# Shorter planned reservations on ScalarE and VectorE, and later planned normalisation for batches 4 to 7

## The chip, the cores and the metric

One core of one Trainium2 chip runs the kernel as one launch. The metric is the device time of that launch in microseconds (us). Timed runs are summed up by their median. One further execution was taken by the hardware profiler, and the rows below come from it.

## The reference, cut to what matters

The computation is an attention without softmax, normalised by a root mean square, followed by two feed-forward blocks. Everything is float32.

```python
kv  = einsum('bhsd,bhse->bhde', k, v)            # 8 batches, 8 heads, 576 tokens, 64 wide
out = einsum('bhsd,bhde->bhse', q, kv)
out = out / sqrt(mean(out * out, -1) + 1e-6) * g_norm
x = out.transpose(0, 2, 1, 3).reshape(4608, 512)
h = x @ w_in;  x = maximum(0.01 * h, h) @ w_out          # first block, 512 -> 2048 -> 512
h = x @ w_in2; return (h - tanh(h)) @ w_out2             # second block, the same sizes
```

## The kernel before

**Stages.** The four large products are done in float16 on TensorE: each operand is split into a high and a low part, and three partial products are added (`three`, L639). Around that sits a scheme that makes a 2 by 2 block product out of seven products instead of eight; it needs sums and differences of operand blocks. After a start of about 60 us, TensorE goes through four stages: `up` of block 1 (eight superblocks of 576 tokens, one for each batch, 56 products each), `down` of block 1, `up` of block 2 and `down` of block 2. Within the first `up` stage the attention of batches 2 to 7 is put between the products, one batch well ahead of the superblock that needs it. A product is counted as one slot; superblock b begins at slot 56 b.

**What an `up` product leaves behind.** ScalarE copies intermediate sums out of PSUM (`keep`, L696, tiles `c`, `u` and a block of `g`), VectorE adds the others (`add`, L707). A PSUM bank is free for a later product only after that, so a late copy on ScalarE holds TensorE up. ScalarE then applies the leaky function to a whole tile `g` (L1265), and it is stored.

**What attention leaves behind.** `pair` computes two heads: `kv` on TensorE (`pk`), copied by ScalarE to `kvd` (L967); q transposed (`pq`), copied by ScalarE to `qt` (L986); the product `po` (L997); its square by ScalarE (L1003) and a copy by VectorE to `xg` (L1012). After the last pair of a batch `norms` runs: ScalarE takes the root (L1056), VectorE the reciprocal (L1064), SyncE stores the result and loads it back spread over the partitions into a tile `bc` (L1067, L1073), twice a batch (kk = 0 and 1). GpSimd multiplies `xg` by `bc` in four pieces for each kk (L1079). Then `left_stages` makes the operands: ScalarE writes the high part `opa` (L576), VectorE its low part (L583), GpSimd four sums (L616), then ScalarE `ops` (L576) and VectorE its low part.

**Other work in the same stretch.** Weights of later stages are converted (`convert`: L432 on ScalarE, L436 to L456 on VectorE) and split (`split_late`: GpSimd sums L498 and L502 on `unit`, ScalarE L518, VectorE L521, tiles `wo`).

**What sets the order.** Every engine executes its instructions in the order in which the kernel emits them. That order is not the order of the loops: a planner (`Plan`) keeps a clock of its own, puts each step on a heap under its planned time and emits the heap in that order. For ScalarE ("A"), VectorE ("V") and GpSimd ("G") it keeps lists of taken stretches. `fit` looks for the first place from time t on where a step of length `dur` goes in, and may overlap its neighbour by `over`. `do` books a single step, mostly the copies out of PSUM, without overlap. `chain` books a row of steps one after another; a step that names no engine only waits, such as a load with the time until it is expected to have landed. The planned end of a step is t + `dur` in both, and `chain` adds `HAND`, 0.25 us. A dry pass over the plan finds products planned before their operands and delays them in the plan. The planned lengths stand in the code, such as 0.438 us for a 288-wide copy out of PSUM on ScalarE (width/1000 + 0.15), 0.486 us for the addition on VectorE (1.2 x width/1000 + 0.14), 1.29 us for the low part of four blocks of 288 on VectorE, 0.79 us for a sum on GpSimd of `xg`.

The plan's clock begins at 0 with the kernel. Its products are set to begin at START, 59.9 us by the constants (the load order and 3 x 6.0 - 3.0), plus what the dry pass adds.

Of the kernel before, what the change touches and what calls it, by code (L numbers as in the profile page):

```python
# [29 lines left out]
NOP = 7  # L30
# [18 lines left out]
class Plan:  # L49
# [2 lines left out]

    HAND, OVER = 0.25, {"A": 0.6, "V": 0.35, "G": 0.35}

    def __init__(self, delays, dry):
# [9 lines left out]
    def fit(self, eng, t, dur, over=0.0):  # L67


        taken = self.taken[eng]  # L70
        k = max(0, bisect.bisect(taken, (t, 0.0)) - 1)
        while k < len(taken) and taken[k][0] < t + dur - over:
            t = max(t, taken[k][1])
            k += 1
        while k < len(taken) and taken[k][0] < t:
            k += 1
        taken.insert(k, (t, t + dur))
        return t
# [125 lines left out]
@with_exitstack  # L204
def body(ctx, tc, *args):
    q, out, w1 = args[0], args[-1], args[4]
    sizes = (*q.shape, *out.shape, w1.shape[1])
    pools = {
        "const": ctx.enter_context(tc.tile_pool(name="const", bufs=1)),
        "wpool": ctx.enter_context(tc.tile_pool(name="wpool", bufs=1)),  # L210
        "work": ctx.enter_context(tc.tile_pool(name="work", bufs=1)),
        "dram": ctx.enter_context(tc.tile_pool(name="dram", bufs=1, space=DRAM)),
        "ps": ctx.enter_context(tc.tile_pool(name="ps", bufs=1, space=PSUM)),
    }
    delays = {}
    unseen = Unseen()
    while True:
        late = lay_out(Plan(delays, True), unseen, {n: unseen for n in pools}, sizes, [unseen] * len(args))
        if late is None:
            break  # L220
        delays[late[0]] = delays.get(late[0], 0.0) + late[1]
    with tc.manual_schedule():
        lay_out(Plan(delays, False), tc.nc, pools, sizes, args)


def lay_out(plan, nc, pools, sizes, args):
    q, k, v, g_norm, w1, w2, w3, w4, out = args
    B, H, S, D, NT, DM, DFF = sizes
    NP = DFF // P // 2
# [18 lines left out]
    def bank(n, name):  # L248
        if n in used:
            plan.miss(("bank", n))  # L250
        used.add(n)
        return ps.tile([P, 512], F32, tag=f"p{n}", name=name)

    def free(n):
        used.discard(n)
        plan.met(("bank", n))
# [570 lines left out]
    LOADBC, LOADBC1 = 8.0, 9.0  # L827
# [119 lines left out]
    def pair(b, c, held):  # L947
# [92 lines left out]
        def m_after(e):  # L1040
            if c == PAIRS[-1]:
                norms(b, e)
# [8 lines left out]
    def norms(b, e):  # L1051
        held = {}

        def root():
            held["iv"] = const.tile([4 * Q, T1], F32, tag="iv", name="iv")
            nc.scalar.activation(  # L1056
                out=held["iv"], in_=pm[b][:4 * Q, :T1], func=AF.Sqrt,
                bias=eps_sb, scale=1.0 / (X_SCALE * X_SCALE),
            )
            free(5)  # L1060

        def inverse(n, m=1):
            part = held["iv"][:, CP * n:CP * (n + m)]
            nc.vector.reciprocal(out=part, in_=part)  # L1064

        def store():
            nc.sync.dma_start(out=ivd[b], in_=held["iv"])  # L1067

        def load(kk):
            held[kk] = L.take([P, 4, T1], F32, "bc", True)  # L1070
            rows = ivd[b].rearrange("(w q) t -> q w t", q=Q)
            for h in range(2):
                nc.sync.dma_start(  # L1073
                    out=held[kk].ap[D * h:D * h + D], in_=rows[2 * kk + h:2 * kk + h + 1].broadcast_to((D, 4, T1))
                )

        def scale(kk, e, n0, n1):
            x = xg[b, kk].ap[:, n0:n1]
            e.tensor_tensor(out=x, in0=x, in1=held[kk].ap[:, n0:n1], op=ALU.mult)  # L1079
            if n1 == 4:  # L1080
                L.give(held[kk])

        x0ops[b] = [{}, {}]
        more = []
        for kk in range(2):
            stages = left_stages(
                lambda kk=kk: xg[b, kk].ap, x0ops[b][kk], None, T1, over=lambda kk=kk: L.give(xg[b, kk]), pieces=2,
                first=None if b else "V", rest=None if b else "V", over_s=() if b else (SOVER,),
            )
            if b == 1:  # L1090
                scaled_ = [("V", 0.66, lambda kk=kk, n=n: scale(kk, nc.vector, n, n + 2)) for n in (0, 2)]
            else:
                scaled_ = [("G", 0.76, lambda kk=kk, n=n: scale(kk, nc.gpsimd, n, n + 1)) for n in range(4 if b else 1)]
            more.append([(None, LOADBC if b > 1 else LOADBC1 if b else 6.0, lambda kk=kk: load(kk))] + scaled_ + stages)

        def wide(kk, n):
            k_ = (4 * kk + n) % 4
            if k_ in used:
                raise NoRoom("bank")
            held["b", kk, n] = bank(k_, "pb")  # L1100
            nc.tensor.matmul(
                out=held["b", kk, n][:, :T1], lhsT=hot["t"].ap[:, kk, n], rhs=held["iv"], start=True, stop=True,
            )

        def scale_wide(kk, n):
            x = xg[b, kk].ap[:, n]
            nc.vector.tensor_tensor(out=x, in0=x, in1=held["b", kk, n][:, :T1], op=ALU.mult)
            free((4 * kk + n) % 4)
            if n == 3:
                if kk == 1:  # L1110
                    L.give(hot["t"])
                plan.chain(plan.now + 0.5, more[kk][2:])

        def split():
            if b == 0:
                for kk in range(2):
                    for n in range(4):
                        plan.chain(
                            plan.now + 0.2 + 0.7 * (4 * kk + n),
                            [(None, 0.9, lambda kk=kk, n=n: wide(kk, n)), ("V", 0.46, lambda kk=kk, n=n: scale_wide(kk, n))],  # L1120
                        )
                return
            for kk in range(2):
                plan.chain(plan.now + (4.5 if b > 1 else 1.8) + 3.0 * kk, more[kk])

        end = plan.do("A", e + 0.15, 1.8, root)
        thirds = [("V", 0.7, lambda n=n: inverse(n)) for n in range(T1 // CP)] if b else [("V", 0.7, lambda n=n: inverse(n)) for n in range(3)]
        plan.chain(end + plan.HAND, thirds + ([(None, 0.0, store)] if b else []) + [(None, 0.0, split)])
# [30 lines left out]
    t = 1.0  # L1159
# [77 lines left out]
    FIRST = {1: (None,) * EARLY + (0, 8, 16, 24)[:4 - EARLY], 2: (14, 25, 36, 47), 3: (60, 72, 84, 96)}  # L1237
# [3 lines left out]
    for b in range(1, B):  # L1241
        for hp in range(4):
            c = PAIRS[hp]
            n0 = FIRST[b][hp] if b in FIRST else NOP * (NP * b - 16 + 2 * hp) - 2 * (b - 4)
            if n0 is None:
                continue
            held = ta[b, c][1] if (b, c) in ta else {}
            for (dur, fn, after), o in zip(pair(b, c, held), OFFS.get(b, (1, 4, 6, 8, 10, 13))):
                extra.setdefault(n0 + o, []).append((dur, fn, after))
            if b > 1:  # L1250
                loads.append((n0 - 13, b, c, held))
# [278 lines left out]
```

## Time and profile before

| | |
|---|---|
| median of 3 runs | 1490.52 us (1490.04 to 1491.99) |
| profiled execution | 1495.29 us |
| its span, first to last instruction | 1493.5 us |
| mean granted clock of TensorE in it | 0.986 of full speed |
| TensorE busy | 1443.8 us, 97% of the span |
| VectorE, ScalarE, GpSimd busy | 1245.4, 933.7, 599.8 us |

A busy TensorE is not the same as TensorE at its peak, since matmuls overlap and their ends are modelled; so the waits and the granted clock are read beside the busy time. A time in brackets behind a row of the timeline is the idle time of that engine just before the row, with what ended it.

### The profile page before, as it was taken

The page shows a single profiled execution, that of the slowest core. Times are in us where ns is not written, and L with a number is a line of the kernel's source. Part 1 is how long each engine was busy: PE and PEld are TensorE (multiplying, and loading weights), DVE is VectorE, ACT ScalarE, POOL GpSimd, SP SyncE. Part 2 cuts the span into 40 slices and gives each one's busy share as a digit, 9 for nine tenths or more (in the row PEclk, how much of TensorE's full clock was granted, in tenths as well). Part 3 has the DMA queues.
Part 4 walks back from the last instruction along what each step waited for, and adds up shares of the span by engine and source line. Part 5 has one row for each costly group of instructions (what it writes and reads, how often), then busy time and mean ns, then how long its engine had stood idle before and what let it go on. Part 6 is the DMA issues. An engine that isn't in the chain of part 4 may idle for free. (4 is left out here: it accounts for less than half of the span.)

```text
span 1493.5 us, 32922 instructions
## 1 busy us (share of the span) xinstructions
PE 1443.8 (97%) x12674; PEld 1195.8 (80%) x12674; DVE 1245.4 (83%) x2029; ACT 933.7 (63%) x1529; POOL 599.8 (40%) x614
## 2 busy tenths in 40 slices
PE   5699999999999999999999999999999999999998
PEld 3467777767777777777777888888888888888887
DVE  4896687677877899999996999989999998888871
ACT  5587777778877644444542677768888555555540
POOL 3141340453643444445542111126577444444430
PEclk8799999999999999999999999999999999999999
DMA  9737898899978745555555856646678744444421
GB/s 281 182 105 228 267 298 263 275 327 306 335 260 300 296 166 191 173 173 200 178 172 198 307 211 221 209 172 221 250 253 320 282 143 154 142 143 146 150 86 36
DMA packets 156461, 321.83 MB, mean 215 GB/s; under 512 B 16656, under 2 KB 98448, under 8 KB 156304
## 3 DMA queue, kind: packets, MB, share of 16 engines
q1 hardware_dynamic: 156304, 319.73, 64.7%
q8 instruction: 99, 1.62, 0.4%
q14 instruction: 58, 0.48, 0.1%
HBM read 189.66 MB, written 130.01 MB: 214 GB/s over the span
## 5 line engine op out<-in xcount | busy, mean ns | idle before, releaser
L639 PEld LDWEIGHTS <-w 128*128 128x128 f16 x8400 | 820.1, 98 | 198.1 <-issue 19.2
L616 POOL TENSOR_TENSOR gl<-gl 128x256 f32<-128x256 f32 (+1 forms) x288 | 322.9, 1122 | 368.3 <-DVE gl L616 132.4
L639 PE MATMUL ps_a<-ops,w 128*128 128x288 f16 (+1 forms) x2400 | 331.7, 282 | 6.5 <-ACT c L696 2.8
L639 PE MATMUL ps_c<-ops,w 128*128 128x288 f16 (+1 forms) x2352 | 314.7, 282 | 2.4 <-DVE g L707 2.3
L639 PE MATMUL ps_a<-opa,w 128*128 128x288 f16 (+1 forms) x2016 | 284.6, 281 | 5.6 <-DVE w L521 4.1
L639 PEld LDWEIGHTS <-ops 128*128 128x128 f16 x1728 | 169.1, 98 | 20.0 <-issue 0.4
L639 PE MATMUL ps_b<-opa,w 128*128 128x288 f16 (+1 forms) x1200 | 175.5, 283 | 0.2 <-DVE r_w L344 0.2
L616 DVE TENSOR_TENSOR gl<-gl 128x288 f32<-128x288 f32 (+1 forms) x256 | 142.4, 558 | 4.3
L616 POOL TENSOR_TENSOR x1g<-x1g 128x256 f32<-128x256 f32 x72 | 69.5, 966 | 172.0 <-PE ps_a L639 109.9
L639 PEld LDWEIGHTS <-opa 128*128 128x128 f16 x1296 | 126.8, 98 | 14.7
L576 ACT ACTIVATE ops<-gl 128x1152 f16<-128x1152 f32 x64 | 74.3, 1161 | 96.2 <-POOL gl L616 96.0
L585 DVE SCALAR_TENSOR_TENSOR ops<-gl,inv,ops 128x1024 f16<-128x1024 f32 x72 | 104.3, 1450 | 28.1 <-ACT ops L578 28.0
L578 ACT ACTIVATE ops<-gl,inv 128x1024 f16<-128x1024 f32 x72 | 82.3, 1144 | 65.7 <-POOL gl L616 65.7
L1432 DVE TENSOR_TENSOR g<-g,th 128x512 f32<-128x512 f32 x144 | 111.9, 787 | 0.9 <-ACT th L1428 0.9
L698 ACT ACTIVATE u<-ps_a,up 128x256 f32<-128x256 f32 x144 | 68.1, 473 | 55.0 <-PE ps_a L639 51.3
L583 DVE TENSOR_TENSOR ops<-gl,ops 128x1152 f16<-128x1152 f32 x64 | 94.2, 1475 | 6.9 <-ACT ops L576 6.9
L707 DVE SCALAR_TENSOR_TENSOR g<-ps_c,u 128x288 f32<-128x288 f32 x128 | 57.9, 452 | 49.2 <-PE ps_c L639 48.5
L639 PE MATMUL ps_c<-w,ops 128*128 128x256 f16 x864 | 97.3, 273 | 0.2 <-DVE osb L707 0.2
L639 PE MATMUL ps_a<-w,ops 128*128 128x256 f16 x864 | 95.8, 273 | 0.0
L1079 POOL TENSOR_TENSOR xg<-xg,bc 128x288 f32<-128x288 f32 x48 | 44.8, 961 | 123.8 <-DMA bc<-iv 55.1
L583 DVE TENSOR_TENSOR opa<-gl,opa 128x864 f16<-128x864 f32 x64 | 81.0, 1266 | 2.0 <-ACT opa L576 1.6
L585 DVE SCALAR_TENSOR_TENSOR opa<-gl,inv,opa 128x768 f16<-128x768 f32 x72 | 79.6, 1106 | 0.8 <-ACT opa L578 0.8
(133 smaller groups left out, 2062.3 us busy)
## 6 DMA issues: line engine op xcount, KB each, us to landing
g<-g SPq DMA_DIRECT2D x64, 576.0 KB, 5.1
gl<-g SPq DMA_DIRECT2D x64, 576.0 KB, 4.5
g<-g SPq DMA_DIRECT2D x72, 512.0 KB, 3.4
gl<-g SPq DMA_DIRECT2D x72, 512.0 KB, 4.2
wd<-wo SPq DMA_DIRECT2D x48, 448.0 KB, 3.4
w<-wd SPq DMA_DIRECT2D x24, 896.0 KB, 8.5
words<-in_moe_w_in_dram SPq DMA_DIRECT2D x64, 256.0 KB, 7.1
words<-in_moe_w_out_dram SPq DMA_DIRECT2D x64, 256.0 KB, 4.5
```

The costliest lines, as they stand in the source:

```text
L576: nc.scalar.activation(out=o, in_=i_, func=AF.Copy)
L578: nc.scalar.activation(out=o, in_=i_, func=AF.Identity, scale=scale())
L583: nc.vector.tensor_tensor(out=o, in0=i_, in1=h, op=ALU.subtract)
L585: nc.vector.scalar_tensor_tensor(out=o, in0=i_, scalar=scale(), in1=h, op0=ALU.mult, op1=ALU.subtract)
L616: lambda: e.tensor_tensor(out=g()[:, o], in0=g()[:, a], in1=g()[:, b], op=op),
L639: nc.tensor.matmul(out=out_, lhsT=a, rhs=c, start=start and m == 0, stop=stop and m == n - 1, skip_group_check=not fresh,)
L698: nc.scalar.activation(out=t, in_=src, func=AF.Identity, scale=self.scale)
L707: nc.vector.scalar_tensor_tensor(out=o, in0=src, scalar=self.minus if sub else self.scale, in1=t, op0=ALU.mult, op1=ALU.add,)
L1079: e.tensor_tensor(out=x, in0=x, in1=held[kk].ap[:, n0:n1], op=ALU.mult)
L1432: nc.vector.tensor_tensor(out=o, in0=o, in1=held["t"].ap[:, 2 * n:2 * n + 2], op=ALU.subtract)
```

## The change

The planner's `fit` gets a factor for each engine. From planned time 130 on it books a step on ScalarE for 0.86 and on VectorE for 0.92 of its length, and scales the allowed overlap alike; GpSimd stays at 1. The planned end of the step, which the next step of a chain waits for, still uses the whole length. For batches 4 to 7 `norms` plans each multiplication on GpSimd with 0.95 instead of 0.76 us, and expects the load of `bc` to have landed after 9.5 instead of 8.0 us. The slot at which a batch's attention begins moves from 2 (b - 4) to 3 (b - 4) slots ahead of its base: one slot sooner for batch 5, two for batch 6, three for batch 7, none for batch 4. No instruction is added or taken away; the order of emission changes.

```diff
+    SETTLED, PITCH = 130.0, {"A": 0.86, "V": 0.92, "G": 1.0}
     HAND, OVER = 0.25, {"A": 0.6, "V": 0.35, "G": 0.35}
@@ def fit(self, eng, t, dur, over=0.0):
         taken = self.taken[eng]
+        if t > self.SETTLED:
+            dur *= self.PITCH[eng]
+            over *= self.PITCH[eng]
         k = max(0, bisect.bisect(taken, (t, 0.0)) - 1)
@@ in norms(b, e)
-                scaled_ = [("G", 0.76, lambda kk=kk, n=n: scale(kk, nc.gpsimd, n, n + 1)) for n in range(4 if b else 1)]
-            more.append([(None, LOADBC if b > 1 else LOADBC1 if b else 6.0, lambda kk=kk: load(kk))] + scaled_ + stages)
+                scaled_ = [("G", 0.76 if b < 4 else 0.95, lambda kk=kk, n=n: scale(kk, nc.gpsimd, n, n + 1)) for n in range(4 if b else 1)]
+            more.append([(None, (LOADBC if b < 4 else LOADBC + 1.5) if b > 1 else LOADBC1 if b else 6.0, lambda kk=kk: load(kk))] + scaled_ + stages)
@@ for b in range(1, B): for hp in range(4):
-            n0 = FIRST[b][hp] if b in FIRST else NOP * (NP * b - 16 + 2 * hp) - 2 * (b - 4)
+            n0 = FIRST[b][hp] if b in FIRST else NOP * (NP * b - 16 + 2 * hp) - 3 * (b - 4)
```

## Rows read from the trace of the kernel before

**Rows 1.** Windows, busy time of each engine by stretch, granted clock, DMA share.

```profile
130.00:200.00 70.00, 67.87 (x616) 51.75 (x613) 45.17 (x94) 51.05 (x107) 14.48 (x16) 0.98 0.87 258
200.00:300.00 100.00, 97.56 (x918) 75.09 (x916) 73.39 (x145) 75.38 (x155) 34.36 (x38) 1.00 0.92 279
300.00:400.00 100.00, 96.37 (x867) 73.26 (x865) 79.05 (x138) 81.11 (x162) 58.27 (x68) 0.98 1.01 325
...
600.00:700.00 100.00, 98.80 (x805) 78.54 (x804) 98.80 (x141) 49.55 (x61) 50.43 (x39) 1.00 0.54 180
...
1100.00:1200.00 100.00, 98.06 (x897) 87.49 (x896) 98.40 (x134) 74.55 (x109) 63.54 (x58) 1.00 0.78 284
1200.00:1300.00 100.00, 100.00 (x919) 89.63 (x917) 88.11 (x113) 51.18 (x62) 45.04 (x45) 1.00 0.44 141
```

**Rows 2.** Timeline of GpSimd, batches 4 and 5: multiplications (L1079) and sums.

```profile
257.20 2.56 POOL L1079 TENSOR_TENSOR xg<-xg,bc 128x288 f32<-128x288 f32 x3 [33.89 <-PE pq L976]
265.78 3.80 POOL L1079 TENSOR_TENSOR xg<-xg,bc 128x288 f32<-128x288 f32 x5 [6.02 <-DMA bc<-iv]
269.52 9.11 POOL L616 TENSOR_TENSOR xg<-xg 128x288 f32<-128x288 f32 x8
...
320.05 6.08 POOL L1079 TENSOR_TENSOR xg<-xg,bc 128x288 f32<-128x288 f32 x6 [4.31 <-DMA bc<-iv]
326.08 1.24 POOL L498 TENSOR_TENSOR unit<-unit 128x256 f32<-128x256 f32 x1
```

**Rows 3.** Timeline of all engines at batch 4.

```profile
268.86 0.92 ACT L576 ACTIVATE opa<-xg 128x864 f16<-128x864 f32 x1 [2.29 <-POOL xg L1079]
...
273.55 1.16 ACT L576 ACTIVATE ops<-xg 128x1152 f16<-128x1152 f32 x1 [2.12 <-POOL xg L616]
...
276.66 0.75 PE L997 MATMUL po<-qt,kvd 128*128 128x288 f32 x2 [1.74 <-ACT qt L986]
```

**Rows 4.** The same at batch 5.

```profile
322.93 0.92 ACT L576 ACTIVATE opa<-xg 128x864 f16<-128x864 f32 x1 [3.41 <-POOL xg L1079]
...
324.20 0.90 PE L639 MATMUL ps_a<-ops,w 128*128 128x288 f16 x6 [0.70 <-ACT c L696]
...
328.92 1.04 ACT L518 ACTIVATE wo<-unit,s_w 128x896 f16<-128x896 f32 x1 [0.56 <-POOL unit L502]
...
330.44 1.09 PE L997 MATMUL po<-qt,kvd 128*128 128x288 f32 x2 [1.90 <-ACT qt L986]
```

**Rows 5.** Windows of 5 us, columns as in the first group.

```profile
165.00:170.00 5.00, 3.22 (x13) 2.19 (x13) 3.64 (x7) 4.31 (x10) 4.84 (x7) 0.69 1.06 301
...
330.00:335.00 5.00, 4.56 (x19) 2.90 (x20) 2.99 (x5) 3.67 (x8) 4.84 (x6) 0.66 1.06 392
```

**Rows 6.** Timeline at batch 6.

```profile
391.86 0.90 PE L639 MATMUL ps_a<-ops,w 128*128 128x288 f16 x6 [0.50 <-ACT u L696]
...
397.47 0.75 PE L997 MATMUL po<-qt,kvd 128*128 128x288 f32 x2 [0.54 <-ACT qt L986]
```

**Rows 7.** Timeline at batch 2, and two neighbouring copies on ScalarE.

```profile
165.37 0.92 ACT L576 ACTIVATE opa<-xg 128x864 f16<-128x864 f32 x1 [4.50 <-POOL xg L1079]
...
166.32 0.41 ACT L696 ACTIVATE c<-ps_a 128x288 f32<-128x288 f32 x1
...
166.63 0.40 ACT L696 ACTIVATE u<-ps_a 128x288 f32<-128x288 f32 x1
166.78 1.54 PE L639 MATMUL ps_a<-ops,w 128*128 128x288 f16 x6 [2.13 <-ACT c L696]
```

**Rows 8.** VectorE groups of 520 to 800 us: count, busy, mean ns, idle before.

```profile
L583 DVE TENSOR_TENSOR ops<-gl,ops 128x1152 f16<-128x1152 f32 x52 | 76.8, 1482 | 5.2 <-ACT ops L576 5.2
...
L616 DVE TENSOR_TENSOR gl<-gl 128x288 f32<-128x288 f32 x100 | 58.3, 585 | 1.2
```

**Rows 9.** The same of 130 to 490 us.

```profile
L616 DVE TENSOR_TENSOR gl<-gl 128x288 f32<-128x288 f32 x16 | 7.2, 451 | 0.1
```

**Rows 10.** Timeline: the longest waits of TensorE behind 500 us.

```profile
684.05 3.10 PE L639 MATMUL ps_a<-ops,w 128*128 128x288 f16 x24 [1.20 <-ACT u L694]
...
1155.51 1.47 PE L639 MATMUL ps_c<-ops,w 128*128 128x256 f16 x12 [1.52 <-DVE g L707]
```

**Rows 11.** TensorE, L639 from 60 to 110 us: durations, first and last start.

```profile
L639 PE MATMUL ps_a<-opa,w x60: 283/286/448, 66.6 to 105.9; 128*128 128x288 f16 x60
```

## The prediction, written before the changed kernel was run

> **What bounds the kernel now.** I read the windows first, stage by stage. TensorE is busy 97 to 100% of every stretch behind 130 us, and at the full granted clock nearly everywhere [rows 1]. The reader is to see there that no other engine sets the pace for long, and that what an order can still win is small. The busy time that is missing in the listed windows is 2.13 us up to 200, 2.44 up to 300, 3.63 up to 400, 1.20 from 600 to 700, 1.94 from 1100 to 1200, and nothing from 1200 to 1300. To it comes the clock: it was 0.69 of full speed in the 5 us from 165 and 0.66 in those from 330, both times just behind a wait of TensorE [rows 5]. Full speed is 2.4 GHz and the lower level 1.2 GHz, so these windows mix both. They cost 5 x 0.31 = 1.55 and 5 x 0.34 = 1.70 us. The listed windows and the two clock drops sum to 11.34 + 3.25 = 14.6 us, 1.0% of the time. The start, before 130, is the larger loss, but the change touches it hardly: the factors begin at 130 on the plan's clock, whose products are set for 59.9 us and a little more, where the trace has them from 66.6 on [rows 11]. So 130 on the plan's clock lies some microseconds behind 130 in the trace.
>
> Next I read the timeline around each wait of TensorE in the first stage. They have one pattern. GpSimd's L1079 runs in groups of eight a batch, the first batch being 2; at batch 4 the first three pieces started at 257.20 and the other five only at 265.78, after 6.02 us of waiting for `bc` [rows 2]. ScalarE, in order, had `opa` of that batch at its head and stood 2.29 us for GpSimd, then 2.12 us for `ops` [rows 3]. Behind it in ScalarE's queue stood the copies of `qt` and the copies out of PSUM, and TensorE waited 1.74 us for `qt` [rows 3]. At batch 5 ScalarE stood 3.41 us for `opa`; TensorE lost 0.70 us for the copy `c`, and a little later 1.90 us for `qt`, behind a `wo` step that GpSimd had late [rows 4]; then came the clock drop at 330 [rows 5]. GpSimd had the sums of `unit` behind six multiplications there, and those behind a wait of 4.31 us for `bc` [rows 2]. Batch 6 shows 0.50 and 0.54 us [rows 6]. Batch 2 shows the worst case of the pattern, 4.50 us on ScalarE and 2.13 on TensorE [rows 7].
>
> **The change, part by part.** No instruction comes or goes; all prices are prices of order.
>
> *Riper batches 4 to 7.* In the plan the step `opa` moves by 1.5 us for the load and 4 x (0.95 - 0.76) = 0.76 us for the multiplications, 2.26 us in all, and so do all steps behind it. A copy out of PSUM is planned at its product and stays. So what fell due up to 2.26 us behind `opa` now goes ahead of it on ScalarE. That is as long as the waits of batch 4 (2.29 and 2.12), so I take its 1.74 us as gone. At batch 5 it covers two thirds of the 3.41 us; the copy `c` that TensorE missed by 0.70 us comes ahead: 0.70 gone. On GpSimd the `unit` sums get ahead of some late multiplications and can run in the 4.31 us of waiting; that would free the 1.90 us and its 1.70 us of clock. But the sums on `xg` are still planned at 0.79 us where the eight of batch 4 took 9.11, 1.14 each [rows 2], so crowding behind them stays. The ends are 0 and 3.60; I take half, 1.80. At batch 6 the ends are 0 and 1.04; I take 0.50. What is late next is the operand itself: the multiplications still wait for the same loads, and the low part of `ops` ends no later than it does now unless GpSimd's order worsens. The cover is that superblock 4 begins at slot 224, while the last pair's final step stands at slot 112 + 42 + 13 = 167: 57 slots stand between, against a chain that grows by 2.26 us, three slots. If that cover were gone, TensorE would stand up to 2.26 us a batch, 9 us over four.
>
> *Sooner attention.* It puts back one to three slots for batches 5 to 7. A product takes six passes of 288 columns, planned at 0.735 us, so 0.7, 1.5 and 2.2 us: about what ripening takes. The loads of k, v and q, 13 slots ahead, go out on SyncE's queue that much sooner, with those of `bc` and the stores in the same queue. The DMA share there was 1.01 [rows 1], so they can make a `bc` load later, but only by their own shift. The steps also meet other products of the cycle of seven. Cost: bounded by the waits of such a meeting, a gain of 0.54 or a loss of 0.70 a batch [rows 4, 6], three batches, -1.6 to +2.1. Nothing in the trace says which sign, so I take 0.
>
> *Shorter bookings.* On ScalarE the trace speaks for them: two copies out of PSUM of 0.41 and 0.40 us started 0.31 us apart [rows 7], and the plan books 0.438, now 0.377. The plan comes nearer to the engine. What it moves is steps of other chains forward by some tenths, ahead of or behind a copy. On VectorE it speaks against them for long steps: the low part of 1152 elements took 1.482 us [rows 8] where the plan books 1.29 and now 1.19. Between 600 and 700 and between 1100 and 1200 VectorE is 98% busy [rows 1]; an addition that falls behind such a step comes later. The trace has no row for a changed order. From below, the gain is what stalls remain: batch 2's 2.13 with 1.55 of clock, and the 1.20 and 1.52 us behind 500 us [rows 7, 5, 10], 6.4 us in all. From above, each addition that is newly caught costs 1.20 to 1.52 us [rows 10]. I take 0, since the tight windows with the larger order (the chains begin at the same times, and VectorE's work is the same) have so far just one such wait each.
>
> A rule speaks against this part. A sum of two SBUF tensors of 288 on VectorE took 451 ns in the first stage, when few GpSimd sums ran beside it, and 585 ns on average later [rows 9, 8]: longer beside GpSimd by 30%. The Trainium skill says in "SBUF — State Buffer", section "Who interferes with whom", that a VectorE instruction with two SBUF inputs contends with a GpSimd instruction that reads SBUF, and that the loser of the shared port pair is fully blocked. By that rule a booking of 0.92 would be too short wherever both run; by the rows the sum above stays, and by the rule it would lose what the third rival below loses.
>
> The sum: 1.74 + 0.70 + 1.80 + 0.50 = 4.74 us off 1495.29 (span 1493.5 and 1.8 around it), so 1490.55. That execution is 0.3% above the median of the runs, 1490.52; the ratio 0.9968 put on the median gives 1485.8, and I say 1486.
>
> **The rivals.** *More is freed.* ScalarE's truer bookings also carry the copy `c` of batch 2 ahead of `opa`. For it speaks that 0.31 us distance; against it that `opa` there is ordered by GpSimd's planned times, which don't change for batch 2. All of batches 4 to 6 (1.74 + 0.70 + 3.60 + 1.04 = 7.08) and batch 2 (3.68) would be 10.8 us: 1480.
>
> *The wait only moves.* ScalarE stands for `opa` as before because GpSimd still stands for `bc`, now one other copy behind it. For it: the loads' landing is not changed, and batch 5's 3.41 exceeds 2.26. Then 1.74 goes and 0.70 comes anew at batch 7, which shows no wait now: 1 us off, 1489.5. This is also how it would look if the change did nothing that TensorE feels.
>
> *VectorE's additions fall behind long steps* (the other side). Place: the first `down` stage and the second `up` stage, where VectorE is 98% busy. Price: 1.36 us each (mean of 1.20 and 1.52). From 4.74 / 1.36 = 3.5 of them on the gain is eaten, and from 5.7 on the kernel is slower by over 3 us. One in each of eight superblocks would be 10.9 - 4.7 = 6.2 us slower, 1497. For it: 1.19 booked against 1.482. Against it: the bookings were too short by 0.19 before, and two waits came of it.
>
> **How the numbers follow.** A measurement tells about 0.2%, 3 us, from no change. My forecast gets 0.50 (its own range 1483.4, all of batches 4 to 6, to 1488.5), more freed 0.13, the wait moves 0.20, VectorE's additions 0.17. About 0.05 of the first lies within 3 us. So faster 0.58, same 0.25, slower 0.17. The range takes the forecast, the moved wait, half of more freed and a part of the last: 1481 to 1494.
>
> **What would show each step.** In the profile after: at batches 4, 5 and 6 ScalarE's waits for L1079 and L616 shrink from 2 to 3.4 us to under 1; TensorE's waits for `qt`, `c` and `u` between 265 and 400 us fall from 5.4 us to under 2; the clock drop at 330 is gone. Batch 2's wait stays. The windows from 600 to 700 and from 1100 to 1200 miss no more of TensorE than the 3.1 us of now. I am wrong if waits for L707 or L694 appear in that stretch, if ScalarE stands for `opa` of batches 4 to 7 as long as before, or if batch 7 shows a wait of TensorE for its operands around the start of its superblock.

## The result, and the profile after

The changed kernel took 1503.12 us (median of 4 runs, 1502.16 to 1504.23) against 1491.26 (4 runs) for the kernel before: a ratio of 1.0078, interval 1.006 to 1.0095. It is slower by 0.8%. The forecast was 1486, the range 1481 to 1494. The profiled execution took 1504.01 us with a span of 1502.2; before it was 1495.29 with 1493.5. Behind `fit` line numbers are 4 higher: L707 is L711, and the three lines of `keep` that copy out of PSUM, L696 in the first `up` stage, L694 in the first `down` stage and L698 in block 2, are now L700, L698 and L702.

The windows of the changed kernel, columns as in [rows 1]: stretch and length, then busy time and count of instructions of TensorE, its weight loads, VectorE, ScalarE and GpSimd, then the granted clock, the DMA share and GB/s.

```profile
130.00:200.00 70.00, 67.01 (x621) 51.27 (x620) 47.02 (x95) 49.51 (x107) 14.29 (x16) 1.00 0.87 265
200.00:300.00 100.00, 98.24 (x921) 75.46 (x919) 74.04 (x149) 75.56 (x161) 34.87 (x39) 1.00 0.93 288
300.00:400.00 100.00, 97.68 (x898) 74.54 (x897) 81.81 (x142) 82.18 (x162) 61.28 (x70) 1.00 1.01 323
...
600.00:700.00 100.00, 96.42 (x773) 76.11 (x771) 96.27 (x139) 46.68 (x58) 48.36 (x37) 0.98 0.55 180
700.00:800.00 100.00, 97.03 (x791) 77.08 (x788) 90.12 (x140) 42.29 (x51) 45.33 (x34) 1.00 0.53 179
...
1000.00:1100.00 100.00, 98.46 (x900) 87.80 (x899) 91.00 (x139) 79.24 (x131) 57.87 (x64) 1.00 0.68 242
1100.00:1200.00 100.00, 93.71 (x851) 82.94 (x849) 95.73 (x131) 71.09 (x108) 58.24 (x55) 1.00 0.76 272
1200.00:1300.00 100.00, 100.00 (x919) 89.63 (x917) 85.84 (x112) 50.17 (x61) 43.88 (x44) 1.00 0.49 150
```

Read against [rows 1]: from 200 to 400 the change gains. TensorE misses 4.08 us there where it missed 6.07. From 130 to 200 it misses 2.99 for 2.13, but the granted clock is 1.00 in all three windows up to 400 where two had 0.98. Behind 500 it loses more than that: the windows from 600 to 700 and from 1100 to 1200 miss 3.58 and 6.29 us where they missed 1.20 and 1.94.

What TensorE waited for from 500 to 1190 us in the changed kernel (total, times, longest):

```profile
PE ps_a L643 <- ACT u L702: 4.2, 4, 1.4
PE ps_a L643 <- DVE opa L587: 3.1, 1, 3.1
PE ps_a L643 <- ACT u L698: 3.0, 2, 2.0
PE ps_a L643 <- ACT c L702: 2.6, 2, 2.1
PE ps_c L643 <- DVE g L711: 1.5, 2, 0.9
PE ps_a L643 <- ACT opa L580: 0.5, 1, 0.5
```

That is 14.9 us. The same view of the kernel before sums to 4.8:

```profile
PE ps_c L639 <- DVE g L707: 1.9, 2, 1.5
PE ps_a L639 <- ACT u L694: 1.8, 2, 1.2
PE ps_a L639 <- ACT c L698: 0.6, 1, 0.6
PE ps_a L639 <- DVE r_w L344: 0.5, 1, 0.5
```

The waits that grew name copies out of PSUM on ScalarE (`u` and `c`: 9.8 us for 2.4) and operands (3.6 us, none before). Those for additions on VectorE (`g`) did not grow: 1.5 us for 1.9. One of the new waits in the timeline:

```profile
1135.08 1.48 DVE L589 SCALAR_TENSOR_TENSOR opa<-gl,inv,opa 128x768 f16<-128x768 f32 x1
1135.09 0.82 PE L643 MATMUL ps_a<-opa,w 128*128 128x256 f16 x6
1135.78 1.15 ACT L582 ACTIVATE ops<-gl,inv 128x1024 f16<-128x1024 f32 x1 [1.81 <-POOL gl L620]
1136.48 0.86 DVE L711 SCALAR_TENSOR_TENSOR g<-ps_c,up,u 128x256 f32<-128x256 f32 x2
...
1136.83 0.45 ACT L702 ACTIVATE u<-ps_a,up 128x256 f32<-128x256 f32 x1
...
1137.34 0.81 PE L643 MATMUL ps_a<-ops,w 128*128 128x256 f16 x6 [1.43 <-ACT u L702]
```

ScalarE has the high part `ops` at its head and stands 1.81 us for GpSimd's sums. The copy `u`, which TensorE waits for, is next in line: 1.43 us lost. On VectorE two additions stand behind the low part `opa` of 1.48 us. It is the pattern that the prediction found at batches 2, 4 and 5 in the first stage [rows 3, 4, 7], now in a stage where it was rare. Seven of the eight late copies stand so, behind a step for an operand or a weight that had itself waited for GpSimd, VectorE or a load. Two more of these steps:

```profile
723.99 1.16 ACT L580 ACTIVATE ops<-gl 128x1152 f16<-128x1152 f32 x1 [3.99 <-POOL gl L620]
...
1179.73 0.94 ACT L582 ACTIVATE opa<-gl,inv 128x768 f16<-128x768 f32 x1 [4.44 <-DMA gl<-g]
```

The dearest wait is in the first `down` stage:

```profile
651.28 1.58 DVE L587 TENSOR_TENSOR ops<-gl,ops 128x1152 f16<-128x1152 f32 x1
652.78 1.64 DVE L587 TENSOR_TENSOR opa<-gl,opa 128x864 f16<-128x864 f32 x1
...
654.48 0.77 PE L643 MATMUL ps_a<-opa,w 128*128 128x288 f16 x5 [3.09 <-DVE opa L587]
```

VectorE did another low part first, and TensorE stood 3.09 us for the second one. The two next windows of 5 us show what followed; 165 and 330 stand beside them for [rows 5]:

```profile
165.00:170.00 5.00, 3.66 (x25) 2.52 (x25) 4.93 (x8) 4.90 (x11) 4.76 (x7) 1.00 0.89 309
330.00:335.00 5.00, 5.00 (x61) 4.24 (x62) 5.00 (x6) 3.38 (x8) 4.84 (x6) 1.00 1.08 282
650.00:655.00 5.00, 1.42 (x12) 0.87 (x10) 5.00 (x6) 2.51 (x4) 3.27 (x2) 1.00 0.66 193
655.00:660.00 5.00, 5.00 (x30) 3.35 (x28) 4.97 (x7) 2.22 (x5) 1.99 (x3) 0.66 0.70 235
```

The clock drops at 165 and 330 are gone, and one of the same size has come at 655, worth 5 x 0.34 = 1.7 us. At batch 4 the operands came as the prediction had it:

```profile
265.23 0.91 ACT L580 ACTIVATE opa<-xg 128x864 f16<-128x864 f32 x1
265.46 4.74 POOL L1083 TENSOR_TENSOR xg<-xg,bc 128x288 f32<-128x288 f32 x5 [7.27 <-DMA bc<-iv]
...
269.59 0.91 ACT L580 ACTIVATE opa<-xg 128x864 f16<-128x864 f32 x1
...
274.88 1.16 ACT L580 ACTIVATE ops<-xg 128x1152 f16<-128x1152 f32 x1 [1.29 <-POOL xg L620]
```

GpSimd still stands for `bc`, 7.27 us where it was 6.02 [rows 2], but ScalarE no longer stands with it for `opa` (2.29 us before, [rows 3]), and the wait for `qt` of 1.74 us is gone. Batch 4 has a new one, 1.34 us for an addition at 278.78. At batch 6 ScalarE has a wait for GpSimd that it did not have before, and at 386.52 TensorE stands 0.89 us for a copy `u`:

```profile
383.84 1.16 ACT L580 ACTIVATE ops<-xg 128x1152 f16<-128x1152 f32 x1 [2.81 <-POOL xg L620]
```

### The profile page after: what moved, and what is told of

It is laid out like the page before. It is cut to its first block, busy times and chain, and to the rows that moved or that the text cites. A ratio compares the mean times of both kernels' runs of the same rounds, so it can differ in the third digit from the quotient of the medians.

```text
span 1502.2 us, 32830 instructions
## 1 busy us (share of the span) xinstructions
PE 1442.7 (96%) x12674; PEld 1193.7 (79%) x12674; DVE 1242.2 (83%) x2029; ACT 927.8 (62%) x1529; POOL 607.5 (40%) x614
## 4 chain that ended last, share of the span: by engine, by line
PE 43%; DVE 9%; issue 3%; POOL 2%; ACT 2%; DMA 1%; DVEq 0%; SPq 0%; POOLq 0%; ACTq 0%
PE ps_a L643 20%; PE ps_c L643 13%; PE ps_b L643 6%; PE ps_d L643 4%; DVE opa L587 2%; DVE g L1436 1%; POOL gl L620 1%; DVE g L711 1%; DVE gl L620 1%; DVE opa L589 1%; DVE wo L525 1%; DMA g<-g 1%; ACT ops L580 1%; DVE ops L589 1%; DVE ops L587 1%
## 5 line engine op out<-in xcount | busy, mean ns | idle before, releaser
L620 POOL TENSOR_TENSOR gl<-gl 128x256 f32<-128x256 f32 (+1 forms) x288 | 329.3, 1144 | 374.6 <-DVE gl L620 140.3
L589 DVE SCALAR_TENSOR_TENSOR ops<-gl,inv,ops 128x1024 f16<-128x1024 f32 x72 | 97.6, 1356 | 8.6 <-ACT ops L582 8.6
L702 ACT ACTIVATE u<-ps_a,up 128x256 f32<-128x256 f32 x144 | 67.9, 472 | 48.2 <-PE ps_a L643 46.2
L711 DVE SCALAR_TENSOR_TENSOR g<-ps_c,u 128x288 f32<-128x288 f32 x128 | 57.8, 452 | 44.3 <-PE ps_c L643 38.7
```

The costliest lines, as they stand in the source:

```text
L589: nc.vector.scalar_tensor_tensor(out=o, in0=i_, scalar=scale(), in1=h, op0=ALU.mult, op1=ALU.subtract)
L620: lambda: e.tensor_tensor(out=g()[:, o], in0=g()[:, a], in1=g()[:, b], op=op),
L702: nc.scalar.activation(out=t, in_=src, func=AF.Identity, scale=self.scale)
L711: nc.vector.scalar_tensor_tensor(out=o, in0=src, scalar=self.minus if sub else self.scale, in1=t, op0=ALU.mult, op1=ALU.add,)
```

## The experiments

Theory V: VectorE's factor 0.92 makes the loss. Theory A: ScalarE's factor 0.86 does. Theory O: any new order in the stages behind 500 us costs. Theory R: the riper batches do it. All kernels start from the changed one; 480 and 812 on the plan's clock lie just ahead of the ends of the first `up` and the first `down` stage. Every ratio is to the kernel before, run on the same chip; e1 to e4, e6 to e9, e10 to e13 and e14 to e17 ran in four groups on three chips, and what is compared between groups are these ratios.

The last column parts the one profiled execution of each run: the first `up` stage from its first product to its last copy L700, the first `down` stage from there to its last copy L698, and the rest up to the end of the span. The kernel before and e1, e4, e11, e14 and e15, which have no factor behind the first stage, agree in the second figure (332.9 to 333.1 us) and in the third (669.3 to 669.7), so a microsecond more there comes from the order. The first figure is less steady: the eight runs with the same factors and batches in the first stage (e4, e6 to e10, e16, e17) have 414.5 to 418.8 us.

| run | first `up` stage | behind it | ratio (interval) | first `up` / first `down` / rest, us |
|---|---|---|---|---|
| kernel before | none | none | 1 | 424.7 / 332.9 / 669.3 |
| changed kernel | both factors, riper, sooner | both factors | 1.0078 (1.006 to 1.0095) | 419.9 / 339.3 / 676.4 |
| e1_ripe_only | riper, sooner | none | 1.0056 (1.0035 to 1.0078) | 432.0 / 333.1 / 669.4 |
| e2_act_only | ScalarE, riper, sooner | ScalarE | 1.0019 (1.0002 to 1.0036) | 417.5 / 334.1 / 673.8 |
| e3_dve_only | VectorE, riper, sooner | VectorE | 1.0097 (1.0069 to 1.0125) | 429.1 / 336.9 / 672.0 |
| e4_first_stage | both, riper, sooner | none | 0.9965 (0.9948 to 0.9981) | 418.2 / 333.0 / 669.7 |
| e6_later_act | as e4 | ScalarE 0.86 | 1.0015 (1.0000 to 1.0029) | 415.7 / 334.1 / 675.4 |
| e7_later_dve | as e4 | VectorE 0.92 | 0.9992 (0.9976 to 1.0008) | 417.4 / 335.5 / 671.7 |
| e8_later_dve_longer | as e4 | VectorE 1.08 | 1.0007 (0.9995 to 1.0018) | 414.5 / 331.6 / 678.4 |
| e9_later_tiny | as e4 | both 0.99 | 0.9966 (0.9952 to 0.998) | 418.8 / 331.8 / 671.1 |
| e10_down_longer | as e4 | VectorE 1.08 in first `down` | 0.9958 (0.9944 to 0.9971) | 415.3 / 331.6 / 669.3 |
| e11_first_not_riper | both factors only | none | 1.0020 (1.0006 to 1.0034) | 426.4 / 332.9 / 669.3 |
| e12_light_full_change | as changed, VectorE lighter | both | 0.9953 (0.9938 to 0.9968) | 417.7 / 332.8 / 668.3 |
| e13_light_first_stage | as e4, VectorE lighter | none | 0.9925 (0.9904 to 0.9946) | 415.9 / 330.5 / 666.4 |
| e14_first_act | ScalarE, riper, sooner | none | 0.9982 (0.9968 to 0.9996) | 420.3 / 333.1 / 669.4 |
| e15_first_dve | VectorE, riper, sooner | none | 1.0054 (1.0037 to 1.007) | 430.4 / 333.0 / 669.3 |
| e16_first_and_down | as e4 | both, first `down` alone | 1.0024 (1.0011 to 1.0036) | 416.5 / 338.8 / 669.5 |
| e17_first_and_up2 | as e4 | both, from second `up` on | 1.0028 (1.0013 to 1.0042) | 417.3 / 332.9 / 677.2 |

### One part at a time, and the first stage alone

e1, e2 and e3 set factors back to 1.0; e4 ends them behind the first stage:

```diff
-    SETTLED, PITCH = 130.0, {"A": 0.86, "V": 0.92, "G": 1.0}
+    SETTLED, PITCH = 130.0, {"A": 1.0, "V": 1.0, "G": 1.0}     # e1;  e2: A 0.86, V 1.0;  e3: A 1.0, V 0.92
@@ e4
-        if t > self.SETTLED:
+        if self.SETTLED < t < 480.0:
```

> Both factors back at 1.0; the riper batches 4 to 7 and their sooner slots stay. Theory V (VectorE's factor 0.92 costs behind 500 us, 10 us of waits): no waits beyond the 4.8 us of the kernel before there, the first stage better by its 3 us, so about 1488. Theory A (ScalarE's factor 0.86 costs): the same, 1488. Theory O (any new order in the stretches where VectorE is near full brings new waits, whatever made it): 1495 to 1505, since the planner delays a product of superblock 6 by 7.6 us on its own clock here and so reorders everything behind it. Theory R (the riper batches themselves do it): 1500 or more.

> The whole change but VectorE's factor 1.0; ScalarE's 0.86 stays. Theory V: the waits behind 500 us go, about 1488 to 1491. Theory A: they stay, about 1503. Theory O: 1495 to 1505, with the waits at other places than in the changed kernel.

> The whole change but ScalarE's factor 1.0; VectorE's 0.92 stays. Theory V: about 1503, waits behind 500 us of some 15 us. Theory A: about 1488 to 1491. Theory O: 1495 to 1505.

> The whole change, but the factors hold only from 130 to 480 on the plan's clock, so in the first up stage alone. If the loss comes from the factors in the later stages (V or A): the first stage keeps its 3 us and the later ones are as before, about 1488. Theory O: a few microseconds above that, since a few steps begun before 480 still stand elsewhere, 1490 to 1493. Theory R: about 1503.

e4 is the clear one. With the factors in the first stage alone the kernel is faster than before by 0.35%, some 5 us, and theory R falls: the loss is the factors' work behind the first stage, 1.0078 - 0.9965 = 1.13%, some 17 us with an uncertainty of 3 to 4. In the profiled executions the two later parts are longer by 6.3 + 6.7 = 13.0 us than in e4. e1 came out slow by another cause, which sits in the first stage: 432.0 us there, and behind it the figures of the kernel before. e3 has both, 429.1 us and 6.2 us more than e4 behind it. The timeline of e1:

```profile
375.13 0.46 DVE L711 SCALAR_TENSOR_TENSOR g<-ps_b,c 128x288 f32<-128x288 f32 x1 [5.20 <-DMA g<-g]
...
378.35 0.90 PE L643 MATMUL ps_c<-ops,w 128*128 128x288 f16 x6 [3.12 <-DVE g L711]
...
407.07 0.28 PE L643 MATMUL ps_a<-ops,w 128*128 128x288 f16 x1 [1.69 <-ACT ops L580]
...
409.76 0.41 PE L643 MATMUL ps_a<-ops,w 128*128 128x288 f16 x2 [2.40 <-DVE ops L587]
```

TensorE stands 1.69 and 2.40 us for the operands `ops` of the superblock that begins there. By its place, two superblocks ahead of the stage's end, it is that of batch 6. ScalarE's two `ops` steps for it start at 401.68 and 405.87 with no idle time before them, so they are late by the planned order and not by a wait; with ScalarE's factor (e14) they start at 382.71 and 396.92. The longest wait has another cause: 3.12 us for an addition, before which VectorE had stood 5.20 us for the store of a tile `g`. So neither e1 nor e3 says anything on the later stages by its whole time alone. e2, at 1.0019, fits none of the theories as they stood; it is near what the runs below give for ScalarE's factor in both places, 0.9982 in the first stage and 0.50% behind it.

### Which factor, behind the first stage

```diff
         if t > self.SETTLED:
-            dur *= self.PITCH[eng]
-            over *= self.PITCH[eng]
+            f = (self.PITCH if t < 480.0 else self.LATER)[eng]
+            dur, over = dur * f, over * f
```

`LATER` is A 0.86, V 1.0 in e6; A 1.0, V 0.92 in e7; A 1.0, V 1.08 in e8; both 0.99 in e9. e10 uses V 1.08 for t below 812 and no factor behind it.

> The first up stage as in the changed kernel; from 480 on the plan's clock ScalarE's factor 0.86 alone. The kernel whose factors end at 480 ran at 0.9965 of the kernel before. Theory V (the loss behind 500 us is VectorE's factor): 0.995 to 0.999. Theory A (it is ScalarE's): 1.003 to 1.009. Theory O (any new order there costs): 1.000 to 1.006.

> The same, but from 480 on VectorE's factor 0.92 alone. Theory V: 1.003 to 1.009. Theory A: 0.995 to 0.999. Theory O: 1.000 to 1.006.

> The same, but from 480 on VectorE's bookings are lengthened by 1.08, ScalarE's are as before the change; the plan then delays two products of the second up stage by 1.55 us each on its own clock. Theory V (too short bookings let additions fall behind long steps): fewer waits than the 4.8 us behind 500 us, 0.993 to 0.9965. Theory O: 1.000 to 1.006 here too.

> The same, but from 480 on both factors 0.99, so that the order changes only a little in kind and no booking by more than 13 ns. Theories V and A, by proportion an eighth or less of the loss: 0.996 to 0.998. Theory O: 1.000 to 1.006, as for any other new order.

Above e4, ScalarE's factor costs 0.50%, VectorE's 0.27%, the lengthened one 0.42% and the tiny ones nothing (0.01%). Theory V in its plain form falls: ScalarE's factor costs at least as much, and lengthening VectorE's bookings did not help over both stages. Theory O in its plain form falls with e9: a new order is not dear in itself. The two factors together cost 1.13%, more than 0.50 + 0.27; with intervals of about 0.15% each, the ratios leave open whether they do more than add up. The stages say where. In the first `down` stage ScalarE's factor alone adds 1.1 us to the 333.0 of e4 and VectorE's 2.5, both together 6.3 (5.8 in e16), so there they do more than add up. Behind it they add 5.7 and 2.0, together 6.7 (7.5 in e17), so there they about add up, and ScalarE's is the larger. Lengthened bookings on VectorE take 1.4 us off the first `down` stage and add 8.7 behind it.

> The first up stage as in the changed kernel; VectorE's bookings lengthened by 1.08 in the first down stage alone (480 to 812 on the plan's clock), no factor behind it. There VectorE's factor has so far moved the waits one way: 4.9 us with 0.92, 2.4 with 1.0, 1.3 with 1.08. If that is its effect: 0.995 to 0.9965, with about 1 us of waits in that stage and 2.4 behind it, and the fastest kernel so far. If those three numbers are chance of order: any from 0.9965 to 1.001.

The waits in the first `down` stage went to about 1 us as expected, the stage took 331.6 us as in e8, and the time is the lowest of all versions of the whole work, 0.9958. That it beats e4 is not shown: the intervals overlap widely. It beats the kernel before and the changed one.

### Is it VectorE's load?

e12 and e13 keep the order of the changed kernel and of e4, instruction by instruction, and make two kinds of VectorE steps short; they leave out most of the row maxima and of the subtraction of tanh, so their times are compared with each other and not as versions of the whole work:

```diff
-        nc.vector.tensor_reduce(out=out_, in_=in_, axis=AX.X, op=ALU.max, apply_absolute_value=True)
+        nc.vector.tensor_reduce(out=out_, in_=in_[:, :32], axis=AX.X, op=ALU.max, apply_absolute_value=True)
@@ tanh, two(n)
-            o = g()[:, 2 * n:2 * n + 2]
+            o = g()[:, 2 * n:2 * n + 2, :64]          # and the other operand alike
```

> The whole change, in the same order, with less work on VectorE behind 500 us: the row maxima read 32 of 288 columns and the subtraction of tanh covers 64 of 256 columns, so both outputs are left partly undone. Theory F (a hastened order costs only because VectorE is full there, so additions queue behind long steps): the waits of 15 us behind 500 us shrink to under 4, about 0.993 to 0.997, and the twin below is no faster than 2 us. Theory P (the order itself holds TensorE up, by waits for GpSimd, loads and products, whatever VectorE's load): still 10 us or more behind the twin.

> The twin: factors in the first up stage alone, with the same work left out on VectorE (row maxima over 32 columns, the subtraction of tanh over 64). Both theories: few waits behind 500 us, 0.992 to 0.996; it is the measure for the run above.

The windows of e12, then of e13:

```profile
600.00:700.00 100.00, 100.00 (x818) 79.88 (x817) 97.14 (x140) 47.72 (x58) 52.83 (x40) 1.00 0.58 192
700.00:800.00 100.00, 97.96 (x798) 77.84 (x797) 87.42 (x156) 43.25 (x53) 44.61 (x34) 1.00 0.50 168
...
1100.00:1200.00 100.00, 98.40 (x902) 88.04 (x900) 83.67 (x130) 70.54 (x103) 48.48 (x52) 1.00 0.75 265
```

```profile
600.00:700.00 100.00, 100.00 (x819) 79.88 (x817) 97.33 (x142) 49.50 (x59) 53.60 (x38) 1.00 0.57 188
700.00:800.00 100.00, 100.00 (x818) 79.75 (x816) 87.64 (x151) 43.36 (x54) 40.96 (x36) 1.00 0.50 170
...
1100.00:1200.00 100.00, 100.00 (x918) 89.64 (x917) 87.89 (x134) 69.41 (x98) 52.02 (x52) 1.00 0.74 267
```

With the order of the changed kernel TensorE now misses 0, 2.04 and 1.60 us in these windows instead of 3.58, 2.97 and 6.29. Between the twins 0.28% is left of 1.13%, some 4 us of 17. That difference is uncertain by 0.26%; in the profiled executions the parts behind the first stage differ by 2.4 + 1.9 = 4.3 us, where the full work has 13.0. So two thirds to three quarters of the loss needed VectorE's load, as theory F says, though it had allowed 2 us for the rest; that rest is in the order itself, as theory P says, and its waits in e12 are for copies `u` and `c` on ScalarE. By what way VectorE's load reaches the copies is not shown. ScalarE's waits for GpSimd's sums do not tell it; from 500 to 1190 us (total, times, longest) they are, in e4, the changed kernel, e13 and e12:

```profile
ACT ops L580 <- POOL gl L620: 94.8, 46, 4.8
ACT ops L580 <- POOL gl L620: 109.8, 46, 5.8
ACT ops L580 <- POOL gl L620: 82.5, 41, 4.7
ACT ops L580 <- POOL gl L620: 98.2, 43, 5.4
```

The later factors add 15.0 us to them with VectorE full and 15.7 with VectorE lighter, but with VectorE lighter less of it holds TensorE up. In the windows from 700 to 800 and from 1100 to 1200 VectorE's busy time fell from 90 and 96% to 87 and 84%; between 600 and 700 it is still 97%, and there the missing time is gone all the same, so busy share alone does not tell where a late step hurts.

### Which stage, and which factor in the first one

```diff
-        if t > self.SETTLED:
+        if self.SETTLED < t < 480.0:                     # e14: A 0.86, V 1.0;  e15: A 1.0, V 0.92
+        if self.SETTLED < t < 812.0:                     # e16
+        if self.SETTLED < t < 480.0 or t > 812.0:        # e17
@@ e11: as e4, and in norms and the loop over the batches
-("G", 0.76 if b < 4 else 0.95, ...
+("G", 0.76, ...
-(LOADBC if b < 4 else LOADBC + 1.5) if b > 1 else
+LOADBC if b > 1 else
-- 3 * (b - 4)
+- 2 * (b - 4)
```

> The factors in the first up stage alone, and batches 4 to 7 neither riper nor sooner. If ripening is what frees the first stage, as the prediction has it: the waits at batches 4 to 6 (5.4 us) and the clock drop come back, 0.999 to 1.002. If the truer bookings on ScalarE do it: 0.995 to 0.998.

> The first up stage alone, riper and sooner batches, with ScalarE's factor 0.86 only. Both factors there ran at 0.9965, none (in all stages) at 1.0056, where TensorE stood 4.1 us for the operands of batch 6. If ScalarE's bookings are what keeps the operands in time: 0.995 to 0.999, no wait for operands at batch 6. If VectorE's are: 1.003 to 1.007.

> The same with VectorE's factor 0.92 only. If ScalarE's bookings keep the operands in time: 1.003 to 1.007 with some 4 us of waiting for the operands of batch 6. If VectorE's: 0.995 to 0.999.

> The whole change, but no factor behind the first down stage. If the loss is that stage's (6.6 us of waits in the changed kernel, 2.4 before, and a clock drop): about 1.001. If both later stages lose alone: 1.000 to 1.002. If only the two together lose: 0.9965.

> The whole change, but no factor in the first down stage. If both later stages lose alone (8.3 us of waits behind 826 us in the changed kernel, 2.4 before): 1.001 to 1.004, and this loss and that of the twin above add up to the 1.1% between 0.9965 and 1.0078. If only the first down stage loses: 0.9965.

Each later stage loses alone: the first `down` stage 1.0024 - 0.9965 = 0.59%, the second `up` stage with what follows 0.63%. They add up to 1.22%, against 1.13% for the whole. In the profiled executions they cost 5.8 and 7.5 us, each in its own part and nothing in the other, against 6.3 and 6.7 for the whole.

In the first stage the parts do not add up. Factors alone: 1.0020; in that trace waits for `qt` at batches 4 and 5 (1.60 and 0.86 us) and for `u` and `qt` at batch 6 (1.97 and 0.92) are back, with a clock of 0.97 from 300 to 400. Riper and sooner alone: 1.0056 (with no factors at all). Both: 0.9965. e14 and e15 tell which factor is needed: with ScalarE's alone 0.9982, with VectorE's alone 1.0054. e15 stands 1.69 and 2.40 us for the same operands as e1, and 3.72 us for the addition; e14 has neither wait, but one of 2.76 us for `qt` at 337.45. VectorE's factor may add 0.17% on top of ScalarE's; the intervals overlap, so this is not shown.

## Why the prediction was wrong

**Shorter bookings: the step that failed.** The prediction took 0 for them, between a gain of 6.4 us and 1.20 to 1.52 us for each addition newly caught. Behind the first stage they cost 1.13%: 0.59% in the first `down` and 0.63% from the second `up` stage on, 6.3 and 6.7 us in the profiled executions. The reason given for 0, that chains begin at the same times and VectorE's work is the same, does not hold: the traces show operand steps on ScalarE ahead of copies, waiting for GpSimd or a load, and TensorE behind the copies (9.8 us for 2.4). Two thirds to three quarters of it went away with VectorE's load (e12 against e13).

**The rival that came, by another way.** It was the third, at 0.17: VectorE's additions behind long steps, in these two stages, where VectorE is 98% busy. The place and the part of VectorE's load are borne out (e16, e17, e12 against e13). The mechanism is not: TensorE's waits for additions fell from 1.9 to 1.5 us, and those that grew are for copies on ScalarE and for operands. The rows that the prediction priced an addition by hold the seed of this: the 1.20 us of [rows 10], in its window from 600 to 700, is a wait for a copy `u` on ScalarE. It blamed the 1.19 us booked against 1.482; but ScalarE's factor, which the trace seemed to speak for [rows 7], costs 0.50% behind the first stage and VectorE's 0.27%. Its price of 10.9 us for eight waits was near: the waits there rose by 14.9 - 4.8 = 10.1 us, and a clock drop of 1.7 came with them, 11.8 of the 13.5 us that the two parts grew over the kernel before.

**Riper batches: the right size, by luck in part and for an incomplete reason.** The sum for batches 4 to 6 was 4.74 us, 0.32%; the first stage alone gave 0.35% (e4). The wait for `qt` at batch 4, both waits at batch 5 and the clock drop at 330 went as forecast. By parts the sum did not come out: in the changed kernel batch 4 lost 1.34 us again for an addition, batch 6 has 1.38 us of waits for the 1.04 before, and the clock drop at 165, which stood outside the sum, is gone with batch 2's wait still there. And the prediction gave all of it to ripening and nothing to ScalarE's bookings. Ripening without them costs (e1, e15), in part since the operands come too late. The prediction named that danger and took 57 slots, worked out for superblock 4, as its cover. By the same count superblock 6 has more, 336 - 273 = 63; the count does not show how late the plan puts the operand steps on ScalarE.

**The signs it named.** ScalarE's waits for `opa` at batches 4 and 5 are gone; for `ops` at batch 4 they are 1.29 and 0.93 us, one of them above the 1 us that was set, and batch 6 has a new one of 2.81. TensorE's waits for `qt`, `c` and `u` from 265 to 400 us are 0.64, 0.89 and 0.49 us, 2.0 for a forecast of under 2. Batch 2's wait stayed, 1.68 us and then 1.31 for `qt`. The windows from 600 to 700 and from 1100 to 1200 were to miss at most 3.1 us and miss 9.9. The waits by which it said it would be wrong there did not bring this: those for L707 are 0.67 us, for 1.93 before, and there is none for L694, for 1.20. These windows miss by operands `opa` (3.58 us) and copies L702 (5.56 us).

**What stays open.** Riper and sooner were not run apart, so the price of the sooner slots, taken as 0, is not known. The ratios put the loss behind the first stage at 17 us, the profiled executions at 13.0; of the eight with the same first stage, e4's ended it last, at 487.2 us where the others have 480.2 to 486.4, so part of the distance is in that stage and not behind it.

What VectorE loses beside GpSimd stands in the last section; what that costs the kernel was not isolated, since lightening VectorE takes away both its load and its meetings with GpSimd.

## What to carry to other kernels

A planned duration that is nearer to the engine in one stage can be wrong for another: ask for each stage what the hastened steps will queue in front of, what they themselves wait for, and whether the fullest engine there has time to spare. A change that acts through a whole schedule is first cut by stage; here a gain of 0.35% and a loss of 1.13% stood in one diff, and one condition on the planned time parts them. Where one engine is nearly full, zero is no safe price for a new order: changed bookings behind the first stage moved its two later parts here by -1.4 to +8.7 us each, and more often up than down.

## What the runs showed of the hardware

The granted clock fell behind TensorE's wait of 3.09 us (0.66 from 655 to 660) and behind those of 2.13 and 1.90 us of the kernel before [rows 5]; behind the 2.01 us at 768 and the 2.06 us at 1183 of the changed kernel the windows of 10 us show 1.00. So not every wait of 2 us cost clock here, and what it adds to a wait had to be read from its own window.

VectorE's sums and low parts, which read two operands in SBUF, were slower while GpSimd ran. In the kernel before, of the 100 sums of [rows 8] the 65 that had no instruction of GpSimd running beside them took 0.449 us on average, 0.460 at most; the other 35 took 0.837. So the 30% between [rows 9] and [rows 8] is a mean over few slow sums and many undisturbed ones. The low part `ops` took 1.346 us alone (25 of them) and 1.596 beside GpSimd (26), against 1.29 planned and 1.19 booked. The sums, with least, median and longest time in ns:

```profile
L616 DVE TENSOR_TENSOR gl<-gl x100: 440/452/1048, 523.2 to 781.9; 128x288 f32<-128x288 f32 x100
```
